# An attention and two feed-forward layers on one core: kept columns for the softmax sums, a third PSUM tile for first products, and second matmuls three chunks behind

## The chip, the cores and the metric

The kernel runs on one core of a Trainium2 chip. The metric is the device time of one execution in microseconds (us), and lower is better. The profile's engines are PE (TensorE matmuls), PEld (its weight loads), DVE (VectorE), ACT (ScalarE), POOL (GpSimd) and SP (SyncE, which issues nearly all DMAs).

## The reference

Three steps follow each other. Attention over 4 batches, 8 heads, 576 tokens and 64 dimensions is the sum of two parts: an attention among averages of 4 tokens, repeated 4 times, and a local one in which a token sees those less than 4 away. Its output, 2304 tokens by 512, goes through two feed-forward layers with 2048 hidden values.

```python
q_d = q.reshape(B, H, Sd, factor, D).mean(axis=3)        # the same for k and v; factor = 4
out_up = np.repeat(sm_attn(q_d, k_d, v_d), factor, axis=2)
mask = np.abs(pos[:, None] - pos[None, :]) < factor
scores = np.where(mask, scale * np.matmul(q, k.transpose(0, 1, 3, 2)), -1000000000.0)
out_local = np.matmul(softmax(scores), v)                # sums get + 1e-09 before the division
x = (out_up + out_local)                                 # as [2304, 512]
h = x @ w_in;  g = np.where(h > 0.0, h, np.exp(np.minimum(h, 0.0)) - 1.0);  x = g @ w_out
h = x @ w_in2; g = s * np.maximum(h, 0.0) ** 2 + b;                         out = g @ w_out2
```

## The kernel before

**Feed-forward.** Both layers are cut into 9 blocks of 256 tokens (j) and 16 chunks of 128 hidden values (f). `ffn_h` computes a chunk's first product, 12 matmuls into a PSUM tile `h` (line 875). ACT, DVE, ACT and POOL then make the nonlinear value as a high part `gh` and a low part `gl`: in layer 1 a Relu and an Exp on ACT (L895, L897), a combination on DVE that reads `h` again (L899), the rounding `gh` on ACT and the rest `gl` on POOL or DVE (L300 is the helper line of every tensor_tensor that may run on either). `ffn_x` multiplies `gh` and `gl` with the second weight, 12 matmuls of 256 columns in layer 1 (L931), 6 of 512 in layer 2 (L934), into two PSUM tiles `acc` that gather over the 16 chunks of a block. `LAG = 2` sets how many chunks the second product comes behind the first. Each weight chunk is loaded as 1 MB in a 64-bit form and converted on DVE, ACT and POOL (L346, L351, L353, L292, L300).

**PSUM.** Of eight tiles, two are `at` (attention), two are `h`, four are `acc`. An `h` tile is free again when DVE's L899 has read it.

**Attention.** A unit is a batch and a pair of heads. Units of batch 0 run before the feed-forward starts, their second half and batch 1 beside the first blocks, batches 2 and 3 (whose local part is done row by row on POOL and DVE, L300, L790 to L819) beside the middle blocks. A unit takes transposes on PE (L512), scores (L550, L639), exponentials on ACT that also give the sums (L571, L667), the reciprocal of the sum on DVE (L577 and L578; L685 and L686; L808 and L809), a multiplication on POOL or DVE, transposes (L595, L698) and the products with v (L612, L713). The averages of v are added on PE in batch 0 (`vsum_pe`, L527) and on POOL or DVE elsewhere (`vsum`, L536 and L537).

**The order of the work.** [...] Where the planner sees PE without work for more than a fraction of a microsecond, it writes filler matmuls into an unused PSUM tile (`keep_warm`, L1135). The constants T0 to VP, GROUP, SWITCH, HOLD and WAIT set due times and choices. For layer 1, blocks 0 and 1 run interleaved at the pace at which weights arrive, blocks 2 to 6 one after the other, blocks 7 and 8 interleaved.

```python
copy(self.vd, ps, 4 * D, r=[ps], w=[self.vd], u=self.tdv, due=due)    # end of vsum_pe
op("dve", 0.29, d2, r=[sm], w=[s4, rs], due=due)                      # sum + 1e-9, times 4; reciprocal
drain(LAG + (ph == 0 and j < 2))
```

Of the kernel before, what the change touches and what calls it, by code (L numbers as in the profile page):

```python
# [16 lines left out]
QB = 96  # L17
# [7 lines left out]
NLP = 3  # L25
# [29 lines left out]
class Plan:  # L55
# [6 lines left out]
    GROUP = 9.0  # L62
    SWITCH = 0.024
    HOLD = 0.089
    WAIT = 1.512
# [162 lines left out]
def attn_moe_moe2(ctx, tc, q, k, v, w_in, w_out, w2_in, w2_out, s2, b2, mask, mask_d, out):  # L228
# [33 lines left out]
    ring = [p1.tile([QB, NQB, 2, D], F32, name=f"p{i}") for i in range(NLP)]  # L262
    nbufs["ring"] = NLP
# [110 lines left out]
    class Unit:  # L374
# [147 lines left out]
        def vsum_pe(self, due):  # L522
            ps = self.ps([G, 4, D], "acc")

            def pe():
                for r in range(4):
                    nc.tensor.matmul(ps(), lhsT=ident[:G, :G], rhs=self.vg()[:, :, r * D:(r + 1) * D],  # L527
                                     start=(r == 0), stop=(r == 3))

            op("pe", 1.9, pe, r=[self.vg], w=[ps], u=self.both, due=due)  # L530
            copy(self.vd, ps, 4 * D, r=[ps], w=[self.vd], u=self.tdv, due=due)

        def vsum(self, due):
            def f(e):
                vg = self.vg()
                e.tensor_tensor(out=vg[:, :, 0:2 * D], in0=vg[:, :, 0:2 * D], in1=vg[:, :, 2 * D:4 * D], op=ALU.add)  # L536
                e.tensor_tensor(out=self.vd(), in0=vg[:, :, 0:D], in1=vg[:, :, D:2 * D], op=ALU.add)  # L537

            op(("pool", "dve"), (2.1, 1.3), (lambda: f(nc.gpsimd), lambda: f(nc.vector)),
               r=[self.vg], w=[self.vg, self.vd], due=due, lock=True)  # L540

        def gs(self, heads, halves, due):
# [11 lines left out]
            nm, sm, s4, rs = (Buf(p2, t, [G, N2, 1]) for t in ("gnm", "gsm", "gs4", "grs"))  # L554
# [25 lines left out]
            op("dve", 0.29, d2, r=[sm], w=[s4, rs], due=due)  # L580
# [4 lines left out]
        def gpt_(self, heads, halves, due):  # L585
# [14 lines left out]
            copy(pt, ps, 2 * n * m * G, r=[ps], w=[pt], due=due)  # L600
# [46 lines left out]
        def softmax(self, pss, half, due):  # L647
            F = 2 * NQB
            n = F * SW
            sc = Buf("ring", "p", None)  # L650
            sc.ring = ring
            part = lambda a: sc()[:, :, a, :SW]
            every = lambda: sc().rearrange("p m a w -> p (m a) w")[:, :, :SW]
            mx, sm, rs = (Buf(p2, t, [QB, F, 1]) for t in ("lmx", "lsm", "lrs"))

            by_act = self.b == 0 and self.hp % 2 < ACT_EXP
            for a, ps in enumerate(pss):
                h = slice(a, F, 2)
                if by_act:
# [22 lines left out]
            def d2():  # L682
                if not by_act:
                    nc.vector.tensor_reduce(out=sm()[:, :, 0], in_=every(), axis=AX.X, op=ALU.add)
                nc.vector.tensor_scalar(out=rs(), in0=sm(), scalar1=1e-9, scalar2=None, op0=ALU.add)  # L685
                nc.vector.reciprocal(out=rs(), in_=rs())  # L686

            op("dve", 0.29 if by_act else 0.5 + n / 960, d2, r=[sc, sm], w=[sm, rs], due=due)
# [16 lines left out]
        def lpv(self, half, due):  # L705
# [10 lines left out]
            op("pe", 0.75, pe, r=[self.vwp[half], self.lpt[half]], w=[ps], u=self.both, due=due)  # L716
# [26 lines left out]
    def direct(b, t, due):  # L743
# [32 lines left out]
        sc = Buf(p2, "ds", [128, 4, 7])  # L776
# [8 lines left out]
        def scores(j):  # L785
# [5 lines left out]
                out=sc()[:, j:j + 2], in_=x(), axis=AX.X, op=ALU.add), r=[x], w=[sc], due=due)  # L791
# [11 lines left out]
        op("dve", 0.35, d1, r=[sc, c_sb2], w=[sc, mx], due=due)  # L803
        op("act", 0.2, lambda: nc.scalar.activation(out=sc(), in_=sc(), func=ACTF.Exp, scale=SCALE), r=[sc], w=[sc], due=due)

        def d2():
            nc.vector.tensor_reduce(out=sm()[:, :, 0], in_=sc(), axis=AX.X, op=ALU.add)
            nc.vector.tensor_scalar(out=sm(), in0=sm(), scalar1=1e-9, scalar2=None, op0=ALU.add)  # L808
            nc.vector.reciprocal(out=sm(), in_=sm())  # L809
            nc.vector.tensor_tensor(out=sc(), in0=sc(), in1=bc(sm), op=ALU.mult)  # L810

        op("dve", 0.75, d2, r=[sc], w=[sc, sm], due=due)

        def values(j):
# [3 lines left out]
               r=[vo, sc], w=[x], u=[rows_], due=due)  # L818
# [45 lines left out]
    def ffn_h(ph, j, f, n=N):  # L864
        due = vt(ph, j, f)
        ps = Buf(ps_h, "h", [128, n])
# [12 lines left out]
        us = 0.0075 + n / 2311  # L879
# [10 lines left out]
        gh, gl = Buf(p3, "gh", [128, n], F32R), Buf(p3, "gl", [128, n], F32R)  # L890
# [3 lines left out]
        if ph == 0:  # L894
            op("act", ta, lambda: nc.scalar.activation(out=e(), in_=ps(), func=ACTF.Relu, scale=-1.0),  # L895
# [300 lines left out]
```

## Time and profile before

| | before |
|---|---|
| median of 3 runs | 994.69 us (989.42 to 995.15) |
| the profiled execution: time | 995.36 us |
| its span, first to last instruction | 993.6 us |
| PE busy in the span | 965.5 us (97%) |
| DVE, ACT, POOL busy | 634.1, 472.2, 405.1 us |
| mean granted TensorE clock | 0.985 |
| filler matmuls (L1135) | 588 |

The span falls into five stretches: from the start to the first matmul of the feed-forward (0 to 52.3 us), layer 1's blocks 0 and 1 (to 227.1), its blocks 2 to 6 (to 484), its blocks 7 and 8 (to 582.2), and layer 2 with the last store (to 993.6). A busy PE is not a PE that does useful work: filler matmuls count, and so do matmuls at half the clock.

### The profile page before, as it was taken

The page shows a single profiled execution, that of the slowest core. Times are in us where ns is not written, and L with a number is a line of the kernel's source. Part 1 is how long each engine was busy: PE and PEld are TensorE (multiplying, and loading weights), DVE is VectorE, ACT ScalarE, POOL GpSimd, SP SyncE. Part 2 cuts the span into 40 slices and gives each one's busy share as a digit, 9 for nine tenths or more (in the row PEclk, how much of TensorE's full clock was granted, in tenths as well). Part 3 has the DMA queues.
Part 4 walks back from the last instruction along what each step waited for, and adds up shares of the span by engine and source line. Part 5 has one row for each costly group of instructions (what it writes and reads, how often), then busy time and mean ns, then how long its engine had stood idle before and what let it go on. Part 6 is the DMA issues. An engine that isn't in the chain of part 4 may idle for free.

```text
span 993.6 us, 21541 instructions
## 1 busy us (share of the span) xinstructions
PE 965.5 (97%) x8480; PEld 893.2 (90%) x8480; DVE 634.1 (64%) x1112; ACT 472.2 (48%) x1227; POOL 405.1 (41%) x358
## 2 busy tenths in 40 slices
PE   8999899998999999999999999999999999999998
PEld 6798888988989989999999999999999999999997
DVE  3478978888898989999637788433333343434332
ACT  4567566436444455444666675433333333333332
POOL 1245554688677787778465563100000000000000
PEclk8599999999999999999999999999999999999999
DMA  9556566435443353333335354001001010100000
GB/s 209 107 150 165 143 180 176 122 108 157 111 105 92 89 132 95 86 106 108 103 105 171 114 169 143 22 1 43 20 25 35 10 43 1 44 1 22 1 23 21
DMA packets 102469, 88.35 MB, mean 89 GB/s; under 512 B 48864, under 2 KB 91872, under 8 KB 102368
## 3 DMA queue, kind: packets, MB, share of 16 engines
q1 hardware_dynamic: 100576, 86.54, 31.4%
q8 instruction: 66, 1.08, 0.5%
q10 hardware_dynamic: 1792, 0.44, 0.2%
q14 instruction: 35, 0.29, 0.1%
HBM read 73.85 MB, written 13.11 MB: 88 GB/s over the span
## 4 chain that ended last, share of the span: by engine, by line
PE 48%; issue 3%; POOL 3%; DVE 3%; ACT 1%; SPq 0%; DMA 0%; POOLq 0%; DVEq 0%; ACTq 0%
PE h L875 24%; PE acc L934 20%; PE acc L931 4%; POOL gl L300 1%; POOL wu L300 1%; POOL w L300 1%; DVE raw L819 1%; DVE raw L351 1%; DVE r L899 0%; ACT raw L292 0%; DVE raw L353 0%; ACT r L895 0%; ACT w L292 0%; DVE wu L300 0%; ACT r L897 0%
## 5 line engine op out<-in xcount | busy, mean ns | idle before, releaser
L875 PE MATMUL h<-x,w 128*128 128x256 f32 x3264 | 430.6, 281 | 13.1 <-DVE r L899 10.8
L875 PEld LDWEIGHTS h<-x,w 128*128 128x128 f32 x3264 | 408.0, 188 | 30.7 <-DVE r L899 13.7
L931 PE MATMUL acc<-gh,w 128*128 128x256 f32 x1152 | 186.1, 283 | 0.0
L934 PE MATMUL acc<-w,gh 128*128 128x512 f32 x576 | 181.0, 395 | 0.0
L931 PEld LDWEIGHTS acc<-gh,w 128*128 128x128 f32 x1152 | 155.0, 188 | 2.5 <-issue 2.3
L905 DVE SCALAR_TENSOR_TENSOR r<-r,sb,h 128x256 f32<-128x256 f32 x144 | 68.8, 479 | 129.7 <-ACT r L904 128.6
L300 POOL TENSOR_TENSOR x<-xr,x 128x256 fp32r<-128x256 f32 (+2 forms) x43 | 43.1, 1021 | 264.0 <-DVE x L294 256.3
L300 POOL TENSOR_TENSOR gl<-r,gh 128x256 fp32r<-128x256 f32 x118 | 113.5, 967 | 59.3 <-ACT gh L292 52.5
L910 DVE SCALAR_TENSOR_TENSOR gl<-r,sb,gh 128x256 fp32r<-128x256 f32 x144 | 73.9, 513 | 99.2 <-ACT gh L908 99.2
L908 ACT ACTIVATE gh<-r,sb 128x256 fp32r<-128x256 f32 x144 | 73.4, 510 | 98.5 <-PE acc L934 89.4
L904 ACT ACTIVATE r<-h 128x256 f32<-128x256 f32 x144 | 55.1, 383 | 134.9 <-PE h L875 133.9
L931 PE MATMUL acc<-gl,w 128*128 128x256 f32 x576 | 114.4, 280 | 0.3 <-POOL gl L300 0.3
L934 PE MATMUL acc<-w,gl 128*128 128x512 f32 x288 | 114.0, 396 | 0.0
L934 PEld LDWEIGHTS acc<-w,gh 128*128 128x128 f32 x576 | 98.2, 188 | 14.1
L895 ACT ACTIVATE r<-h 128x256 f32<-128x256 f32 x144 | 54.7, 380 | 96.5 <-PE h L875 47.2
L300 POOL TENSOR_TENSOR w<-raw,w 128x512 fp32r<-128x512 f32 x47 | 64.2, 1379 | 78.7 <-ACT w L292 74.1
L899 DVE SCALAR_TENSOR_TENSOR r<-r,h 128x256 f32<-128x256 f32 x144 | 58.0, 412 | 49.4 <-ACT r L897 47.2
L931 PEld LDWEIGHTS acc<-gl,w 128*128 128x128 f32 x576 | 87.8, 188 | 0.9 <-POOL gl L300 0.7
L292 ACT ACTIVATE gh<-r 128x256 fp32r<-128x256 f32 x144 | 58.2, 413 | 52.6 <-DVE r L899 32.7
L934 PEld LDWEIGHTS acc<-w,gl 128*128 128x128 f32 x288 | 54.0, 188 | 13.0
L300 POOL TENSOR_TENSOR wu<-raw 128x896 f32<-128x896 f32 x29 | 61.5, 2135 | 9.3 <-DVE raw L819 9.3
L819 DVE TENSOR_REDUCE raw<-wu 128x128 f32<-128x896 f32 x36 | 63.5, 1783 | 2.1 <-POOL wu L300 2.0
(136 smaller groups left out, 1149.3 us busy)
## 6 DMA issues: line engine op xcount, KB each, us to landing
raw<-in_moe_w_in_dram SPq DMA_DIRECT2D x32, 512.0 KB
raw<-in_moe_w_out_dram SPq DMA_DIRECT2D x32, 512.0 KB
raw<-in_k_dram SPq DMA_DIRECT2D x17, 320.0 KB
raw<-in_v_dram SPq DMA_DIRECT2D x17, 320.0 KB
x2d<-ev SPq DMA_DIRECT2D x18, 256.0 KB
xr<-x2d SPq DMA_DIRECT2D x18, 256.0 KB
out_dram<-ev SPq DMA_DIRECT2D x16, 256.0 KB
vg<-in_v_dram SPq DMA_DIRECT2D x12, 288.0 KB
```

What stands on the lines that cost most here:

```text
L292: a = (0.11 + n / 1200, lambda: nc.scalar.activation(out=out(), in_=src(), func=ACTF.Copy, scale=scale))
L300: f = lambda e: lambda: e.tensor_tensor(out=out(), in0=in0(), in1=in1(), op=alu)
L819: op("dve", 0.07 + 14 * D / 546, lambda: nc.vector.tensor_reduce(out=vo()[:, WD + j * D:WD + (j + 2) * D].rearrange("p (j d) -> p j d", j= ...
L875: nc.tensor.matmul(ps(), lhsT=w()[:, wpart, 0, c * 128:(c + 1) * 128], rhs=x()[:, xpart, c, :], start=first and i == 0, stop=last and i == ...
L895: op("act", ta, lambda: nc.scalar.activation(out=e(), in_=ps(), func=ACTF.Relu, scale=-1.0), r=[ps], w=[r1], u=[e], due=due)
L899: op("dve", td, lambda: nc.vector.scalar_tensor_tensor(out=e(), in0=e(), scalar=-1.0, in1=ps(), op0=ALU.add, op1=ALU.max), r=[r2, ps], w=[ ...
L904: op("act", ta, lambda: nc.scalar.activation(out=e(), in_=ps(), func=ACTF.Relu), r=[ps], w=[r1], u=[e], due=due)
L905: op("dve", td + 0.07, lambda: nc.vector.scalar_tensor_tensor(out=e(), in0=e(), scalar=sb2[:, 0:1], in1=ps(), op0=ALU.mult, op1=ALU.mult), ...
L908: op("act", ta + 0.1, lambda: nc.scalar.activation(out=gh(), in_=e(), func=ACTF.Identity, bias=sb2[:, 1:2]), r=[r2], w=[gh], u=[e], due=due)
L910: op("dve", td + 0.07, lambda: nc.vector.scalar_tensor_tensor(out=gl(), in0=e(), scalar=sb2[:, 1:2], in1=gh().bitcast(F32), op0=ALU.add, o ...
L931: nc.tensor.matmul(acc()[:, c * N:(c + 1) * N], lhsT=wo[:, cc * 128:(cc + 1) * 128], rhs=g(), start=(f == 0 and i == 0 and c == 0), stop=l ...
L934: nc.tensor.matmul(acc(), lhsT=g()[:, a * 128:(a + 1) * 128], rhs=wo, start=(f == 0 and i == 0), stop=last)
```

## The change

Five things change. The rows of PE, DVE and POOL behind the words were read from the instruction lists that both programs build.

- The sums of the softmaxes are written into column 0 of tiles of two columns (`gsm`, `lsm`), or lie beside a column that nothing else writes (`ds`, `p`). The kept column holds 1e-9 from the start. One tensor_reduce over both replaces the tensor_scalar that added 1e-9 (L577, L685, L808 go, L580 and others come). The factor 4 moves into a copy (`scale=0.25`), and the scaling of the negative maximum moves from DVE (L563) to ACT (L569).
- Batch 0's averages of v move from PE (`vsum_pe`, L527) to POOL or DVE (`vsum`).
- In blocks 2 to 6 of layer 1, for f of 3, 6, 9 and 12, the first product goes into an `acc` tile in place of an `h` tile.
- `LAG` is 3 in place of 2, and `gh`, `gl` have four buffers in place of three.
- The planner's constants are others, and tiles `p` of the local softmax are two in place of three.

```diff
-T0, P0, LB, TR, R0, P1, P2 = 39.33, 5.045, 7, 29.37, 2.362, 2.546, 2.787
+T0, P0, LB, TR, R0, P1, P2 = 39.86, 4.909, 5, 35.22, 2.175, 2.551, 2.783
...
-    GROUP = 9.0
-    SWITCH = 0.024
+    GROUP = 18.61
+    SWITCH = 0
...
+    rings = {"p": [p1.tile([QB, NQB, 2, D], F32, name=f"p{i}") for i in range(NLP)],
+             "gsm": [p1.tile([G, 2, 2], F32, name=f"gsm{i}") for i in range(2)],
+             "lsm": [p1.tile([QB, 2 * NQB, 2], F32, name=f"lsm{i}") for i in range(2)],
+             "ds": [p1.tile([128, 4, 8], F32, name=f"ds{i}") for i in range(2)]}
...
             def d2():
-                nc.vector.tensor_scalar(out=s4(), in0=sm(), scalar1=1e-9, scalar2=4.0, op0=ALU.add, op1=ALU.mult)
+                nc.vector.tensor_reduce(out=s4()[:, :, 0], in_=sm()[:, :N2], axis=AX.X, op=ALU.add)
                 nc.vector.reciprocal(out=rs(), in_=s4())
...
+                    if j == 0 and sc != 1.0:
+                        nc.scalar.activation(out=nm(), in_=nm(), func=ACTF.Copy, scale=sc)
...
-        ps = Buf(ps_h, "h", [128, n])
+        third = ph == 0 and 2 <= j < NSUB - LASTP and 3 <= f < FC - 3 and f % 3 == 0
+        ps = Buf(ps_a, "acc", [128, n]) if third else Buf(ps_h, "h", [128, n])
...
-        gh, gl = Buf(p3, "gh", [128, n], F32R), Buf(p3, "gl", [128, n], F32R)
+        gh, gl = Buf(p4, "gh", [128, n], F32R), Buf(p4, "gl", [128, n], F32R)
...
-            u.gs((0, 1), first, d), u.ls(0, d), u.vsum_pe(d + VP)
+            u.gs((0, 1), first, d), u.ls(0, d), u.vsum(d + VP)
...
-    LAG = 2
+    LAG = 3
```

Three places on PE show what the new order does. The first lies in the start, about 14 us into the run: `w_224` and `w_287` hold v of the first and second unit, other `w` tiles hold batch 0's q, k and what is made of them. Before:

```order
L698 MATMUL at<-ident,p_85 128x96 x3
L527 MATMUL acc<-w_224,ident 72x256 x4
L550 MATMUL acc<-w_293 72x144 x2
L512 MATMUL at<-ident,w_150 128x96 x3
...
L512 MATMUL at<-ident,w_150 128x96 x3
L527 MATMUL acc<-w_287,ident 72x256 x4
L595 MATMUL h<-ident,s 72x72 x4
```

The rows L527 are gone, the second unit's scores (L550) have moved ahead of what stood before L527, and a few fillers stand where the list waits for the next unit. The same place, changed:

```order
L523 MATMUL at<-ident,w_163 128x96 x6
L550 MATMUL acc<-w_303 72x144 x2
L598 MATMUL h<-ident,s 72x72 x4
...
L699 MATMUL at<-ident,p_85 128x96 x3
...
L1139 MATMUL h<-wz 128x128
...
L550 MATMUL acc<-w_374 72x144 x2
```

The second place is the passage from blocks 0 and 1 to block 2, whose first matmuls use the weight chunk `w_702` before and `w_840` in the changed list. Before:

```order
L713 MATMUL at<-pt,vw 64x32 x18
L502 MATMUL at<-ident,nat 128x72 x4
L931 MATMUL acc<-gh,w_3150 128x256 x4
L931 MATMUL acc<-gl,w_3150 128x256 x2
L550 MATMUL at<-d 72x144 x4
L875 MATMUL h<-x,w_702 128x256 x12
L875 MATMUL h<-x,w_855 128x256 x12
```

In the changed list the second products of block 1 are all done earlier, and fillers (L1139) stand between the attention's matmuls in their place, 81 ahead of block 2's first matmul and 20 within its first chunk:

```order
L935 MATMUL acc<-gh,w_3055 128x256 x4
L935 MATMUL acc<-gl,w_3055 128x256 x2
...
L1139 MATMUL acc<-wz 128x128
...
L714 MATMUL at<-pt,vw 64x32 x18
L513 MATMUL at<-ident,nat 128x72 x4
...
L550 MATMUL at<-d 72x144 x4
...
L879 MATMUL h<-x,w_840 128x256 x8
```

The third place is in the middle of block 2. In the changed list every third first product goes to `acc`, so that the next product into the same `h` tile comes one chunk later:

```order
L879 MATMUL acc<-x,w_1813 128x256 x12
L550 MATMUL at<-d 72x144 x4
L935 MATMUL acc<-gh,w_904 128x256 x4
...
L879 MATMUL h<-x,w_1955 128x256 x12
...
L879 MATMUL h<-x,w_2090 128x256 x12
...
L879 MATMUL acc<-x,w_2232 128x256 x12
```

The second product comes later too: that of block 2's second chunk (`w_904`) stands behind the first product of the seventh chunk (`w_1813`), and before it (`w_855`) stood behind that of the sixth.

Counts in the two lists, of filler matmuls: ahead of the first feed-forward matmul 153 before and 187 changed; from there to the first second product 61 and 76; from there to block 2's first matmul 315 and 155; behind it 59 and 142. Tensor_tensor rows of the helper line: 309 on POOL and 88 on DVE before, 323 and 74 changed.

## Rows read from the trace of the kernel before

**Rows 1.** The page: span and busy time of each engine.
```profile
span 993.6 us, 21541 instructions
PE 965.5 (97%) x8480; PEld 893.2 (90%) x8480; DVE 634.1 (64%) x1112; ACT 472.2 (48%) x1227; POOL 405.1 (41%) x358
```
**Rows 2.** Busy time by stretch: length, engines, PEclk, DMA share, GB/s.
```profile
0.00:52.30 52.30, 49.35 (x598) 38.55 (x599) 22.13 (x64) 26.34 (x104) 12.20 (x23) 0.71 0.75 165
52.30:227.10 174.80, 165.28 (x2306) 152.77 (x2304) 145.11 (x279) 103.90 (x294) 103.92 (x96) 1.00 0.54 145
227.10:484.00 256.90, 247.91 (x2143) 239.64 (x2142) 232.53 (x362) 126.24 (x370) 194.39 (x157) 1.00 0.42 110
582.20:993.60 411.40, 407.37 (x2624) 367.81 (x2622) 170.95 (x332) 154.12 (x334) 35.29 (x34) 1.00 0.10 34
```
**Rows 3.** PE's timeline in layer 2: start, length, instruction.
```profile
702.41 1.56 PE L875 MATMUL h<-x,w 128*128 128x256 f32 x12
...
705.21 1.56 PE L875 MATMUL h<-x,w 128*128 128x256 f32 x12
```
**Rows 4.** PE's timeline in the start.
```profile
14.92 3.48 PE L527 MATMUL acc<-w,ident 72*72 72x256 f32 x8
...
26.43 2.13 PE L713 MATMUL h<-pt,w 38*64 38x32 f32 x36
...
42.89 3.78 PE L1135 MATMUL at<-wz 128*128 128x128 bf16 x40
...
52.33 0.95 PE L875 MATMUL h<-x,w 128*128 128x256 f32 x6
...
58.75 0.71 PE L931 MATMUL acc<-gh,w 128*128 128x256 f32 x4
```
**Rows 5.** Stretches of one granted clock in the start; columns as in rows 2.
```profile
15.50:45.70 30.20, 30.20 (x295) 21.48 (x294) 12.39 (x38) 15.87 (x68) 7.13 (x10) 0.50 0.70 155
45.70:58.75 13.05, 13.05 (x225) 12.35 (x224) 6.81 (x11) 5.82 (x18) 4.97 (x7) 1.00 0.48 162
```
**Rows 6.** Groups by line: instructions, busy us, mean ns, idle before.
```profile
L527 PE MATMUL acc<-w,ident 72*72 72x256 f32 x32 | 14.4, 631 | 0.0
L536 POOL TENSOR_TENSOR vg<-vg 72x512 f32<-72x512 f32 x10 | 15.6, 1558 | 0.0
L537 POOL TENSOR_TENSOR vd<-vg 72x256 f32<-72x256 f32 x10 | 9.2, 921 | 1.1 <-PE at L612 0.4
```
**Rows 7.** PE's timeline between 90 and 96 us: fillers at the full clock.
```profile
92.40 3.08 PE L1135 MATMUL at<-wz 128*128 128x128 bf16 x52
95.31 0.42 PE L698 MATMUL at<-ident,p 96*128 96x96 f32 x3
```
**Rows 8.** PE's waits from 52 to 582 us: total, times, longest.
```profile
PE h L875 <- DVE r L899: 10.8, 15, 2.3
PE at L698 <- POOL p L300: 3.7, 4, 1.3
```
**Rows 9.** The same waits on DVE between 227 and 484 us alone.
```profile
PE h L875 <- DVE r L899: 7.5, 10, 2.3
```
**Rows 10.** Lines on DVE and one on ACT: ns of one as least, median, most.
```profile
L577 DVE TENSOR_SCALAR gs<-gsm x32: 144/577/1559, 12.1 to 410.2; 72x2 f32<-72x2 f32 x32
L801 DVE TENSOR_TENSOR ds<-ds,dmx x18: 186/188/1128, 193.6 to 465.2; 128x28 f32<-128x28 f32 x18
L807 DVE TENSOR_REDUCE dsm<-ds x18: 167/176/183, 194.3 to 465.9; 128x4 f32<-128x28 f32 x18
```
**Rows 11.** Groups by line: ACT's first step of a chunk, and what it waited for.
```profile
L895 ACT ACTIVATE r<-h 128x256 f32<-128x256 f32 x144 | 54.7, 380 | 96.5 <-PE h L875 47.2 <-POOL gl L300 40.0 <-DVE gl L300 6.5
```
**Rows 12.** The timeline from the last product for block 2's tokens to its first matmul.
```profile
212.26 1.24 PE L713 MATMUL at<-pt,vw 38*64 38x32 f32 x36
...
224.74 0.71 ACT L292 ACTIVATE x<-xr 128x256 fp32r<-128x256 f32 x2
...
227.10 3.30 PE L875 MATMUL h<-x,w 128*128 128x256 f32 x24
```

More of the change, by code (lines that the diff above doesn't have):

```diff
@@ L261, in attn_moe_moe2, with kept @@
     msk = p1.tile([QB, 2, NQB, SW], BF16, name="msk")
-    ring = [p1.tile([QB, NQB, 2, D], F32, name=f"p{i}") for i in range(NLP)]
-    nbufs["ring"] = NLP
+    rings = {"p": [p1.tile([QB, NQB, 2, D], F32, name=f"p{i}") for i in range(NLP)],
+             "gsm": [p1.tile([G, 2, 2], F32, name=f"gsm{i}") for i in range(2)],
+             "lsm": [p1.tile([QB, 2 * NQB, 2], F32, name=f"lsm{i}") for i in range(2)],
+             "ds": [p1.tile([128, 4, 8], F32, name=f"ds{i}") for i in range(2)]}
+    for tag, tiles in rings.items():
+        nbufs[tag] = len(tiles)
+    def kept(tag):
+        b = Buf(tag, tag, None)
+        b.ring = rings[tag]
+        return b
     mskd = p1.tile([128, 2, 28], BF16, name="mskd")
@@ L553, in gs @@
             op("pe", 0.25 * N2 / len(heads) + 0.1, pe, r=[self.d], w=pss, u=self.tdv, due=due)
-            nm, sm, s4, rs = (Buf(p2, t, [G, N2, 1]) for t in ("gnm", "gsm", "gs4", "grs"))
+            nm, s4, rs = (Buf(p2, t, [G, N2, 1]) for t in ("gnm", "gs4", "grs"))
+            sm = kept("gsm")
             e = Buf(p2, "s", [G, N2, 2 * G])
@@ L682, in d2 @@
             def d2():
-                if not by_act:
-                    nc.vector.tensor_reduce(out=sm()[:, :, 0], in_=every(), axis=AX.X, op=ALU.add)
-                nc.vector.tensor_scalar(out=rs(), in0=sm(), scalar1=1e-9, scalar2=None, op0=ALU.add)
+                x = sm() if by_act else sc().rearrange("p m a w -> p (m a) w")[:, :, :SW + 1]
+                nc.vector.tensor_reduce(out=rs()[:, :, 0], in_=x, axis=AX.X, op=ALU.add)
                 nc.vector.reciprocal(out=rs(), in_=rs())
-            op("dve", 0.29 if by_act else 0.5 + n / 960, d2, r=[sc, sm], w=[sm, rs], due=due)
+            op("dve", 0.34 if by_act else 0.34 + n / 960, d2, r=[sc, sm] if by_act else [sc], w=[rs], due=due)
             tt(every, every, lambda: rs().to_broadcast([QB, F, SW]), ALU.mult, n, r=[sc, rs], w=[sc], due=due)
@@ L917, in ffn_x @@
         w = w_b[ph, f]
-        due = vt(ph, j, f) + 2 * (P1 if ph == 0 else P2)
+        due = vt(ph, j, f) + 3 * (P1 if ph == 0 else P2)
         if f == 0:
@@ L1140, in attn_moe_moe2 @@
         nc.vector.memset(wz, 0.0)
-        for t in ring:
+        for t in rings["p"]:
             nc.gpsimd.memset(t, 0.0)
+        for t in rings["gsm"] + rings["lsm"] + rings["ds"]:
+            nc.gpsimd.memset(t, 1e-9)
+        for t in rings["p"]:
+            nc.gpsimd.memset(t[:, :, :, SW:SW + 1], 1e-9)
         make_identity(nc, ident)
```

72 lines of the change are left out of this document (33 added, 39 removed).

## The prediction

> **What bounds the kernel now.** I read the page first, then the busy times by stretch, PE's timeline and last its waits. The page has PE busy 97% of 993.6 us [rows 1], which says little, since fillers count. Layer 2 says more: a chunk starts every 705.21 − 702.41 = 2.80 us [rows 3], its 144 chunks make 403 us, and the stretch from 582.2 us holds nearly nothing else. There PE is the bound and nothing in the change shortens it; the last 4 us are the last store. So whatever comes or goes lies in the first 582 us. Layer 1's 144 chunks cost PE the same 403 us there; the other 179 us are the start (52.3 us), attention matmuls, fillers and waits.
>
> In the start PE is never idle from 15.5 us on, but at half the clock: 30.2 us at a granted 0.50 [rows 5]. Four groups of L527 lie there, 14.4 us together [rows 4, 6]. In blocks 0 and 1 DVE is busy 145.1 and POOL 103.9 of 174.8 us, PE runs many fillers, and the pace is that of the chains through DVE, ACT and POOL [rows 2]. In blocks 2 to 6 PE and DVE are close together, 247.9 and 232.5 of 256.9 us [rows 2]; what PE waits for there is DVE's L899, which frees the `h` tile: 7.5 us in 10 waits [rows 9].
>
> **The change part by part.** Its own base is the profiled execution, 995.36 us (1.76 us around its span); the median of the runs shown is 994.69 us, 0.7 lower. I take the two as one.
>
> *Averages of v off PE.* 14.4 us of matmuls leave the start [rows 6]. They lay on the path: PE had no idle time between 15.5 us and the first second product at 58.75 [rows 4, 5]. Against that the new list has 34 more fillers ahead of the first feed-forward matmul and 15 more from there to the first second product. At half the clock a filler costs 3.78 / 40 = 0.095 us [rows 4], so 49 of them give back 4.6, and 9.8 us is the most that PE alone can win. Those fillers mark places where the list waits for the softmax chain, and a chain through ACT, DVE and POOL is not sped up by a PE that is free earlier; the least is nothing. I take 6 us, nearer to PE's sum, because PE's row has no gap at all there. What replaces L527 is a pair on POOL of 1.56 + 0.92 us [rows 6], four times; POOL is busy 12.2 of the first 52.3 us [rows 2], so it is hidden. Without that cover each pair would cost up to 2.5 us.
>
> *The order in blocks 0 and 1.* From the first second product to block 2 the fillers fall from 315 to 155. At the full clock 52 take from 92.40 to 95.31, 0.056 us each [rows 7]: 160 × 0.056 = 9.0 us less. Behind that they rise from 59 to 142: 83 × 0.056 = 4.6 us more, most of it at the passage to block 2. A filler's time is a wait that the list foresaw; where the wait is still there, it comes back under another name (below). Ends: 0 and 9.0; I take all of it and count new waits apart.
>
> *The passage to block 2.* Before, 227.10 − 212.26 = 14.8 us lie between the last product for block 2's tokens and its first matmul [rows 12], with second products and attention in between. In the new list I count some 12.3 us of PE work and fillers there (L713 at 1.24 us, second products at 0.7 us a half chunk, 81 fillers). If the way through the store, the reload and the split needs all of 14.8, PE waits 2.5 us; if it was slack, nothing. I take 1.2 us more.
>
> *Kept columns.* L577 has a median of 577 ns and a least of 144, a tensor_reduce of like size 176 and never more than 183 [rows 10]. 32 of them save about 32 × (0.57 − 0.18) = 12 us of DVE, and 50 instructions of the same kind go from other softmaxes. DVE ran nearly full beside PE, so this is slack rather than time: no term by itself. The 16 scalings that move to ACT are small, and ACT is busy 472 of 993.6 us [rows 1].
>
> The list also moves 14 tensor_tensors from DVE to POOL, 194.4 of 256.9 us busy in blocks 2 to 6 [rows 2]. Here a row speaks against the change: L801, a tensor_tensor of 28 elements, takes 186 ns or up to 1128 [rows 10], so something holds it too. [...]
>
> *Third tile and LAG.* In blocks 2 to 6 an `h` tile is now needed again after three first products in place of two for most chunks, that is 2.8 us later, and the longest wait on L899 was 2.3 us [rows 9]. Of the 7.5 us I take 5 as gone, since the first and last chunks of a block still have two tiles; ends 0 and 7.5. The waits outside, 10.8 − 7.5 = 3.3 us [rows 8, 9], stay. `LAG = 3` alone is nothing: PE hardly waits for `gl`, and in layer 2 the matmuls stay the same.
>
> *New waits.* An order with other neighbours brings waits of its own; PE's others were 3.7 us on POOL's `p` and a few more [rows 8]. With fewer fillers to stand in front of them I add 2 us, from 0 to 9 (all of the fillers' gain).
>
> Sum: −6 − 9.0 + 4.6 + 1.2 − 5 + 2 = −12.2 us. 995.4 − 12.2 = 983.2, so 983 us.
>
> **The rivals.**
> - *The start stays.* The softmax chain, not PE, sets the first feed-forward matmul. For it: the new fillers stand between attention rows. Against it: no idle time on PE from 15.5 to 58.75 us. 983 + 6 = 989 us.
> - *The third tile does nothing*, the change then not doing what it says: ACT's L895 waited 40.0 us for POOL's `gl`, since `r` has two buffers [rows 11], and that limit stays. Against it: PE's waits are put down to L899, not to L895. 983 + 5 = 988 us.
> - *Fillers become waits.* The pace in blocks 0 and 1 is that of weights and softmaxes, and 9.0 us come back as idle time. DVE's 145 of 174.8 us speak against a full bound. 983 + 9 = 992 us less the 2 already counted, 990.
> - *The clock stays up.* If PE keeps the full clock through the start, the 30.2 us at 0.50 shrink; L713 takes 1.24 in place of 2.13 us [rows 4, 12]. After L527's removal some 16 us of half-clock work are left, half of which is 8 us: 975 us.
> - *The clock stays down: slower.* The granted clock fell at 15.5 us, after a PE with gaps, and came back at 45.7, behind L527 and 40 fillers without a gap [rows 4, 5]. With L527 gone PE has more gaps, and the clock may come back only in block 0, or fall again. Each microsecond at half the clock costs half a microsecond of PE's work; from 24 us more of it the 12 us are eaten, and if it lasted through the first half of blocks 0 and 1 (40 us more) the time is 983 + 20 = 1003 us. Against it: 36 and 37 fillers stand at the first feed-forward matmuls, and from 45.7 us on the clock never fell. [...]
>
> **How the numbers follow.** Forecast 0.45 (977 to 988); the start stays 0.13; the third tile does nothing 0.12; fillers become waits 0.10; the clock stays up 0.10; the clock stays down 0.10. The range 972 to 992 takes in all but the last and the outer parts of the bounds. One per cent, about what a measurement of this kernel can tell from no change, is 984.7 to 1004.6. Faster by more takes seven tenths of the forecast (0.32), the clock that stays up (0.10) and a tenth of the other rivals (0.04): 0.46. Slower by more is the half of the last rival that lasts longest: 0.05. Within it the rest, 0.49.
>
> **What would show it.** First second product near 52 to 53 us in place of 58.75. No PE row of `vsum`, four POOL pairs ahead of 30 us. Fillers in PE's stretch of blocks 0 and 1 halved, and idle time there not up by more than 3 us. The wait on the DVE line of the combination, 7.5 us in blocks 2 to 6, down to 2 or 3. The tensor_reduce on `gsm` at about 0.17 us with no spread. An idle time ahead of block 2's first matmul under 3 us. Wrong it would be made by a clock that comes back after 55 us, or by blocks 2 to 6 that take longer than 257 us.

## The result, and the profile after

The changed kernel takes 977.49 us (median of 4 runs, 976.09 to 980.28), the kernel before beside it 992.06 (4 runs, 985.87 to 995.15): a ratio of 0.9852 with a 95% interval of 0.9804 to 0.9900, 1.5% faster. About half of the gain goes with the clock, as the experiments show. The forecast was 983 us, in a range of 972 to 992. The profiled execution after takes 976.13 us against 995.36 before, 19.2 less.

The page after, span and busy time [rows 1]:

```profile
span 974.0 us, 21374 instructions
PE 955.4 (98%) x8420; PEld 892.2 (92%) x8420; DVE 612.4 (63%) x1058; ACT 473.0 (49%) x1239; POOL 409.2 (42%) x385
```

PE loses 10.1 us of busy time and 9.5 us of idle time, DVE 22 us of busy time. Next, busy time by stretch after, with the columns of [rows 2]: the start, blocks 0 and 1, blocks 2 to 6, and what follows the first second product of layer 2 (its first matmul, where the last row of [rows 2] begins, is at 555.97 us here).

```profile
0.00:35.20 35.20, 31.98 (x601) 28.14 (x602) 20.72 (x59) 24.07 (x105) 17.01 (x36) 1.00 0.99 202
35.20:204.30 169.10, 161.89 (x2232) 150.00 (x2230) 143.11 (x258) 108.86 (x310) 103.83 (x98) 1.00 0.58 162
204.30:453.00 248.70, 247.01 (x2118) 240.75 (x2115) 210.21 (x338) 123.00 (x364) 189.13 (x159) 1.00 0.40 105
566.77:974.00 407.23, 403.17 (x2546) 363.62 (x2544) 164.51 (x319) 147.89 (x318) 32.58 (x36) 1.00 0.10 33
```

The start is 17.1 us shorter and its granted clock 1.00 in place of 0.71; blocks 0 and 1 are 5.7 shorter, blocks 2 to 6 8.2, with PE's idle time there down from 9.0 to 1.7 us; in blocks 0 and 1 it falls from 9.5 to 7.2. PE's timeline after, at the places of [rows 4] and [rows 3], and the clock of the stretches of [rows 5]:

```profile
24.44 1.24 PE L714 MATMUL h<-pt,w 38*64 38x32 f32 x36
...
35.20 0.96 PE L879 MATMUL h<-x,w 128*128 128x256 f32 x6
...
43.40 0.73 PE L935 MATMUL acc<-gh,w 128*128 128x256 f32 x4
...
694.43 1.60 PE L879 MATMUL h<-x,w 128*128 128x256 f32 x12
...
697.27 1.60 PE L879 MATMUL h<-x,w 128*128 128x256 f32 x12
```
```profile
15.50:45.70 30.20, 29.09 (x524) 25.83 (x518) 21.94 (x48) 20.61 (x86) 18.02 (x20) 1.00 0.87 205
45.70:58.75 13.05, 12.15 (x243) 11.08 (x243) 9.61 (x24) 11.09 (x44) 5.43 (x6) 1.00 0.31 106
```

Two things stand here that the prediction's sum did not hold. The granted clock stays at 1.00 up to the last matmul (970 us; 0.56 in the last 2 us of the span, when PE has none): the local products with v take 1.24 us, not 2.13. And a chunk of layer 2 takes 697.27 − 694.43 = 2.84 us, not 2.80.

The first second product of layer 1 and the first of layer 2 cut both executions into three, and the next fence gives the middle part, layer 1, from the kernel before and from the one after (length, then PE busy):

```profile
58.75:590.06 531.31, 510.19 (x5245) 488.34 (x5242) 444.37 (x720) 295.60 (x797) 360.67 (x303) 1.00 0.46 126
```
```profile
43.40:566.77 523.37, 512.52 (x5179) 493.19 (x5177) 420.59 (x674) 298.19 (x811) 353.16 (x310) 1.00 0.45 127
```

The start gives 58.75 − 43.40 = 15.35 us and layer 1 7.94. What follows takes 4.06 back (995.36 − 590.06 = 405.30 before, 976.13 − 566.77 = 409.36 after): together 19.2. In layer 1 PE's idle time falls by 10.3 us (21.1 to 10.9) and its fillers from 374 to 297, which is 4.3 us at 0.056; yet its busy time rises by 2.3, so 6.6 us of work came from elsewhere. Over 144 chunks that is 0.046 us each, about as much as a chunk of layer 2 loses: the matmuls of layer 1 seem slower too, which e6 bears out below.

PE's waits in layer 1 after, as in [rows 8], and the lines that took the place of [rows 6] and [rows 10]: averages of v on POOL, the sum over kept columns, and the two on `ds` (ns as least, median, most):

```profile
PE h L879 <- DVE r L903: 3.7, 7, 0.8
PE at L699 <- POOL p L311: 2.4, 5, 0.8
```
```profile
L536 POOL TENSOR_TENSOR w<-w x4: 1261/1263/1266, 9.1 to 22.5; 72x512 f32<-72x512 f32 x4
L537 POOL TENSOR_TENSOR w<-w x4: 722/725/788, 10.4 to 23.9; 72x256 f32<-72x256 f32 x4
L580 DVE TENSOR_REDUCE gs<-gsm x32: 131/144/155, 12.8 to 378.7; 72x2 f32<-72x4 f32 x32
L804 DVE TENSOR_TENSOR ds<-ds,dmx x18: 186/197/1173, 174.4 to 444.9; 128x28 f32<-128x28 f32 x18
L810 DVE TENSOR_REDUCE dsm<-ds x18: 159/185/186, 176.2 to 445.4; 128x4 f32<-128x32 f32 x18
```

The wait for DVE falls from 10.8 to 3.7 us and that for `p` from 3.7 to 2.4. POOL's pairs are done by 24.6 us. The sum has lost its spread; L804, the tensor_tensor, has kept its own.

### The profile page after: what moved, and what is told of

It is laid out like the page before. It is cut to its first block, busy times and chain, and to the rows that moved or that the text cites. A ratio compares the mean times of both kernels' runs of the same rounds, so it can differ in the third digit from the quotient of the medians.

```text
span 974.0 us, 21374 instructions
## 1 busy us (share of the span) xinstructions
PE 955.4 (98%) x8420; PEld 892.2 (92%) x8420; DVE 612.4 (63%) x1058; ACT 473.0 (49%) x1239; POOL 409.2 (42%) x385
## 4 chain that ended last, share of the span: by engine, by line
PE 69%; DVE 11%; POOL 6%; issue 6%; DMA 4%; ACT 3%; SPq 1%; POOLq 0%; DVEq 0%; ACTq 0%
PE h L879 31%; PE acc L938 21%; PE acc L935 12%; POOL gl L311 2%; PE acc L879 2%; DVE raw L362 2%; DMA raw<-in_moe_w_out_dram 2%; DVE raw L364 2%; POOL w L311 1%; POOL wu L311 1%; DVE raw L357 1%; DVE w L311 1%; DVE raw L822 1%; DVE r L903 1%; DMA w<-in_k_dram 1%
## 5 line engine op out<-in xcount | busy, mean ns | idle before, releaser
L879 PE MATMUL h<-x,w 128*128 128x256 f32 x3024 | 407.0, 284 | 4.0 <-DVE r L903 2.9
L879 PEld LDWEIGHTS h<-x,w 128*128 128x128 f32 x3024 | 387.0, 188 | 19.1 <-DVE r L903 5.0
L935 PE MATMUL acc<-gh,w 128*128 128x256 f32 x1152 | 188.8, 285 | 0.0
L935 PEld LDWEIGHTS acc<-gh,w 128*128 128x128 f32 x1152 | 157.3, 189 | 2.6 <-issue 1.9
L311 POOL TENSOR_TENSOR x<-xr,x 128x256 fp32r<-128x256 f32 (+2 forms) x47 | 40.9, 892 | 262.5 <-DVE x L305 254.6
L914 DVE SCALAR_TENSOR_TENSOR gl<-r,sb,gh 128x256 fp32r<-128x256 f32 x144 | 77.8, 541 | 101.8 <-ACT gh L912 101.8
L908 ACT ACTIVATE r<-h 128x256 f32<-128x256 f32 x144 | 55.0, 382 | 130.2 <-PE h L879 129.8
L311 POOL TENSOR_TENSOR w<-raw,w 128x512 fp32r<-128x512 f32 x48 | 66.5, 1397 | 60.3 <-ACT w L303 55.8
L903 DVE SCALAR_TENSOR_TENSOR r<-r,h 128x256 f32<-128x256 f32 x124 | 50.7, 414 | 54.3 <-ACT r L901 49.3
L899 ACT ACTIVATE r<-h 128x256 f32<-128x256 f32 x124 | 46.8, 378 | 66.3 <-PE h L879 39.0
L901 ACT ACTIVATE r<-r 128x256 f32<-128x256 f32 x144 | 60.0, 417 | 3.9
```

The source lines that it names most:

```text
L311: f = lambda e: lambda: e.tensor_tensor(out=out(), in0=in0(), in1=in1(), op=alu)
L879: nc.tensor.matmul(ps(), lhsT=w()[:, wpart, 0, c * 128:(c + 1) * 128], rhs=x()[:, xpart, c, :], start=first and i == 0, stop=last and i == ...
L901: op("act", ta, lambda: nc.scalar.activation(out=e(), in_=e(), func=ACTF.Exp, scale=-1.0), r=[r1], w=[r2], u=[e], due=due)
L903: op("dve", td, lambda: nc.vector.scalar_tensor_tensor(out=e(), in0=e(), scalar=-1.0, in1=ps(), op0=ALU.add, op1=ALU.max), r=[r2, ps], w=[ ...
L914: op("dve", td + 0.07, lambda: nc.vector.scalar_tensor_tensor(out=gl(), in0=e(), scalar=sb2[:, 1:2], in1=gh().bitcast(F32), op0=ALU.add, o ...
L935: nc.tensor.matmul(acc()[:, c * N:(c + 1) * N], lhsT=wo[:, cc * 128:(cc + 1) * 128], rhs=g(), start=(f == 0 and i == 0 and c == 0), stop=l ...
```

## The experiments

**How times are compared.** The time of every version moves with the mean granted clock of its run. In 57 runs of the kernel before beside the experiments, ten with a mean clock of 0.996 or more have a median of 984.67 us, 31 between 0.980 and 0.990 one of 995.06, and seven below that one of 999.01: 7.6 us for each hundredth. So the table gives the median of all runs, the ratio to those runs of the kernel before that stood beside them (4, 17 or 23 runs), and beside it the median of the runs with 0.996 or more ("clock up").

| kernel | median, us (runs) | ratio, 95% interval | clock up, us (runs) | layer 2, us per chunk |
|---|---|---|---|---|
| before | 994.80 (57) | | 984.67 (10) | 2.80 |
| after | 977.49 (4) | 0.9852 [0.9804, 0.9900] | 976.11 (2) | 2.84 |
| e1 two behind in layer 2 | 979.91 (6) | 0.9878 [0.9823, 0.9933] | 977.00 (3) | 2.84 |
| e2 no third tile | 978.32 (6) | 0.9876 [0.9816, 0.9935] | 977.54 (3) | 2.84 |
| e3 one sum as before | 978.41 (6) | 0.9865 [0.9813, 0.9917] | 977.22 (4) | 2.84 |
| e4 averages on PE | 989.97 (12) | 0.9973 [0.9935, 1.0011] | 987.00 (5) | 2.84 |
| e5 tiles moved by 32 bytes | 973.70 (6) | 0.9849 [0.9803, 0.9895] | 973.70 (6) | 2.82 |
| e6 tiles moved by 192 bytes | 972.76 (6) | 0.9824 [0.9771, 0.9876] | 967.09 (2) | 2.80 |
| e7 before, averages on POOL | 989.03 (12) | 0.9977 [0.9939, 1.0016] | 985.49 (5) | 2.80 |
| e8 before, more fillers | 988.80 (12) | 0.9989 [0.9956, 1.0021] | 987.76 (5) | 2.80 |
| e9 before, tiles moved | 1000.55 (12) | 1.0050 [1.0015, 1.0086] | 991.87 (1) | 2.84 |
| e10 r alone moved by 192 | 975.99 (6) | 0.9829 [0.9785, 0.9873] | 972.88 (3) | 2.83 |
| e11 e6 with old numbers | 979.37 (6) | 0.9835 [0.9797, 0.9873] | 973.57 (1) | 2.80 |
| e12 e6, two behind in both | 973.07 (6) | 0.9795 [0.9759, 0.9831] | 972.34 (2) | 2.80 |

### Why layer 2 is slower: e1, e5, e6, e9, e10

The first suspect was `LAG`. e1 takes it back in layer 2 alone (and the due times of its second products with it):

```diff
-        drain(LAG + (ph == 0 and j < 2))
+        drain((LAG if ph == 0 else 2) + (ph == 0 and j < 2))
```

> The changed kernel with its second products in layer 2 two chunks behind again (layer 1 keeps three; PE's order is the same up to the end of layer 1). In layer 2 the changed kernel takes 2.84 us per chunk against 2.80 before. Theory A (three behind is what slows the first products there): 2.80 us per chunk again, 144 x 0.04 = 5.8 us less, about 972 us. Rival B (the slower pace comes from where the tiles lie in SBUF, which stays): 2.84 us, about 977 us, no change. Rival C (three behind hides gl): new waits on gl in layer 2, slower than 979 us.

The pace stays. In e1's timeline the row between the first two shown holds two chunks (24 matmuls), so from the first to the second are three chunks:

```profile
696.72 1.60 PE L879 MATMUL h<-x,w 128*128 128x256 f32 x12
...
705.24 1.60 PE L879 MATMUL h<-x,w 128*128 128x256 f32 x12
...
708.08 1.12 PE L879 MATMUL h<-x,w 128*128 128x256 f32 x8
```

From 696.72 to 705.24 are 8.52 us, 2.84 for each chunk. Theory A falls. What else differs there is where the tiles lie: the change takes one `p` ring and two small tags out of the pools ahead of them and adds three rings, so that `x` starts at byte 183520 of a partition, before at 184736; that is 224 and 416 bytes behind a multiple of 1024, and `r` lies likewise. e5 and e6 put unused bytes ahead of them, and change nothing else:

```diff
+    pad = p1.tile([128, 8], F32, name="pad")     # e5; e6: [128, 48]
     mskd = p1.tile([128, 2, 28], BF16, name="mskd")
```

> The changed kernel with 32 unused bytes per partition ahead of the tiles of the later pools, so that the tokens' tile x starts at 183552 in place of 183520 (a multiple of 256) and r, gh and gl move with it; every engine's order is the same. Layer 2's slower pace stayed with second products two behind, so LAG isn't its cause. Theory A (where these tiles lie in SBUF sets the pace of the first products): 2.80 us per chunk or less in layer 2 in place of 2.84, about 970 us where the clock holds. Rival B (the place by 32 bytes doesn't matter): 2.84 us and 976 to 978 us.

> As the run before with 192 bytes: x and r come to lie as before the change, 416 bytes behind a multiple of 1024 (x at 183712, before at 184736); gh and gl don't (928 against 160). Theory A1 (the place of x or r): 2.80 us per chunk in layer 2, about 970 us. Theory A2 (the place of gh and gl): 2.84 us, 976 to 978 us, while the shift by 32 may do either. Rival B (not the place, but the four gh and gl): both shifts stay at 2.84 us.

With 192 bytes the chunk is back at 2.80 us, and the profiled execution takes 966.82 us, 9.3 less than after, at nearly the same clock (1.000 and 0.999). e6's timeline and, below it, its layer 1 between the same two marks:

```profile
700.04 1.56 PE L880 MATMUL h<-x,w 128*128 128x256 f32 x12
...
702.84 1.56 PE L880 MATMUL h<-x,w 128*128 128x256 f32 x12
```
```profile
43.38:562.21 518.83, 504.06 (x5179) 484.11 (x5177) 420.32 (x674) 297.75 (x811) 353.34 (x310) 1.00 0.46 129
```

Layer 1 takes 4.5 us less and what follows 4.8 less (966.82 − 562.21 = 404.61 against 409.36). PE's busy time in layer 1 falls by 8.5, but it then waits 3.9 more: part of the slower matmuls had lain over waits. `gh` and `gl` lie 928 bytes behind a multiple of 1024 here and 160 before, so theory A2 falls as far as it says that they alone set the pace. 32 bytes give less than the half, 2.82; from the first to the second of these rows of e5's are five chunks:

```profile
695.86 1.60 PE L880 MATMUL h<-x,w 128*128 128x256 f32 x12
...
709.98 1.60 PE L880 MATMUL h<-x,w 128*128 128x256 f32 x12
```

Two more runs ask whether the place alone does it, and which tile's. e9 moves the tiles of the kernel before to the bad place, e10 moves `r`, `gh` and `gl` of the changed kernel and leaves `x`:

```diff
+    pad = p1.tile([128, 208], F32, name="pad")   # e9, in the kernel before
     mskd = p1.tile([128, 2, 28], BF16, name="mskd")
```
```diff
+                    p2.tile([128, 24], F32, tag="pad", name="pad")   # e10, ahead of the first r
```

> The kernel before, in the same order, with 832 unused bytes per partition ahead of the later pools, so that x and r lie 224 bytes behind a multiple of 1024, as in the changed kernel, in place of 416. Theory A (the change moved x or r to a worse place, and that cost it some 9 us): 2.84 us per chunk in layer 2 in place of 2.80, 990 to 993 us where the clock holds (before: 982.3 at full clock) and 1002 to 1005 at the usual mean clock. Rival B (the place matters only beside what else the change did): 2.80 us, the times of before.

> The changed kernel with 192 unused bytes between x and r: r, gh and gl lie as in the run with all of them moved by 192, x stays at 224 behind a multiple of 1024; same order. Theory A (it is x, which the first products stream): 2.84 us per chunk, 975 to 977 us at full clock. Rival B (it is r): 2.80 us, 966 to 967 us at full clock.

e9's chunks in its timeline, then two of its windows, the last part of the start and layer 1:

```profile
691.89 1.60 PE L876 MATMUL h<-x,w 128*128 128x256 f32 x12
...
694.73 1.60 PE L876 MATMUL h<-x,w 128*128 128x256 f32 x12
```
```profile
30.00:45.70 15.70, 15.02 (x205) 13.91 (x204) 11.05 (x15) 7.62 (x26) 7.84 (x9) 0.78 0.77 182
...
48.77:581.44 532.67, 518.22 (x5245) 497.90 (x5242) 442.12 (x720) 296.26 (x797) 360.62 (x303) 1.00 0.46 125
```

The kernel before gets the slow pace from 832 unused bytes: rival B falls. It costs 4.9 us in what follows layer 1 (991.68 − 581.44 = 410.24 against 405.30). In layer 1 8.0 us more of busy time cover 6.7 of waits; the 1.4 that are left may be clock, since 3.4 us of layer 1 ran at a granted 0.50 there (from 89.0 us).

e10's chunks come next. Below them stand groups of matmuls in layer 1 (100 to 560 us; the second number is the mean ns of one), each time after, e10 and e6: first products, whose operand of 128x256 is `x`, and second products, whose one is `gl`. The weight, 128x128, is loaded by PEld in both (LDWEIGHTS, 188 ns each after).

```profile
693.98 1.60 PE L879 MATMUL h<-x,w 128*128 128x256 f32 x12
...
705.30 1.59 PE L879 MATMUL h<-x,w 128*128 128x256 f32 x12
```
```profile
L879 PE MATMUL acc<-x,w 128*128 128x256 f32 x240 | 32.7, 285 | 0.0
L879 PE MATMUL acc<-x,w 128*128 128x256 f32 x240 | 32.6, 284 | 0.0
L880 PE MATMUL acc<-x,w 128*128 128x256 f32 x240 | 32.0, 282 | 0.0
L935 PE MATMUL acc<-gl,w 128*128 128x256 f32 x534 | 107.2, 282 | 0.0
L941 PE MATMUL acc<-gl,w 128*128 128x256 f32 x534 | 106.0, 279 | 0.0
L936 PE MATMUL acc<-gl,w 128*128 128x256 f32 x544 | 107.8, 279 | 0.0
```

From 693.98 to 705.30 us are four chunks, 2.83 us each, nearer theory A: with `x` unmoved the first products of layer 2 take 1.59 to 1.60 us, as after, and about three quarters of the loss stay. In layer 1 its second products are as fast as e6's (279 ns), while its first ones are nearly as slow as after's (284 and 285). So in these groups each product's pace goes with the place of its operand of 128x256: `x` for the first, `gl` for the second. `x` was not moved alone, and `r`, `gh` and `gl` only together. That the place sets the pace is shown; by what mechanism is not.

### The start, the averages and the clock: e4, e7, e8

e4 puts the averages back on PE in the changed kernel, e7 takes them off PE in the kernel before, and e8 holds them there with fillers ahead:

```diff
-            u.gs((0, 1), first, d), u.ls(0, d), u.vsum(d + VP)
+            u.gs((0, 1), first, d), u.ls(0, d), u.vsum_pe(d + VP)      # e4; e7 the other way round
...
             def pe():
+                for r in range(16):                                     # e8
+                    nc.tensor.matmul(ps().rearrange("p r d -> p (r d)")[:, 0:128], lhsT=wz[:, :G], rhs=wz, start=True, stop=True)
```

> The changed kernel with the averages of v in the first block on PE again (the 32 matmuls and the 4 evictions of before, in an order that the planner makes for it: 106 fillers ahead of the first feed-forward matmul in place of 187). [...] Rival B (the softmax chain sets the start): first feed-forward matmul within 3 us of 35.2, clock at full speed, 977 to 981 us. Rival C (PE's work alone, 7 us at full clock, and no fall of the clock): about 984 us.

> The kernel before with the averages of v in the first block on POOL and nothing else of the change (the planner makes its own list: 201 fillers ahead of the first feed-forward matmul, 578 up to the second sixteen chunks, 708 in all). Theory A (the averages are the change's gain, 8.5 us at full clock by the run that put them back): 973 to 977 us where the clock holds. Rival B (the gain needs the new list of tasks too, since this one has 120 fillers more and they stand for waits): 980 to 985 us where it holds. In both, falls of the clock add up to 10 us; the median is 3 to 6 us above.

> The kernel before with 16 further fillers (bf16, 128 columns, some 0.9 us) ahead of each of the four groups of averages on PE, else in the same order: 3.6 us more work for PE in the start at full clock. Theory A (the clock falls there since PE has gaps and small matmuls, and fillers hold it): mean granted clock 0.995 or more in most runs, in place of 0.985, and 984 to 988 us in place of 995. Rival B (fillers there don't hold the clock): mean clock 0.985 or less, 997 to 1002 us.

e4 is slower by 11 us where the clock is up, nearest rival C, but not by the averages alone. Its first second product is at 47.90 us, 4.5 later than after, of which up to 3.4 are clock (6.8 us at a granted 0.50, from 36.8 us). Its layer 1 takes 582.29 − 47.90 = 534.39 us, 11.0 more than after, with 463 fillers in place of 297 (9.3 us) and 3.4 us at 0.50: the planner (`Plan.emit`, which writes every engine's list ahead, from costs and due times) made another list.

e7 is the other side. Where the clock is up it comes out at 985.49, as before, near its rival B. Its first second product is at 47.06 us. e9, the order of before with as long a stretch at 0.50 in its start (6.8 us), has it at 48.77, so the averages alone give 1.7 us there. e7's list has 49 fillers more in layer 1 (423 for 374), 2.7 us, which is enough to take that back. The window of its layer 1 is 9.1 us longer than before, but most of this may be clock, since 17 us of it ran at 0.50 (its mean clock is 0.98):

```profile
47.06:587.51 540.45, 520.78 (x5293) 497.85 (x5291) 447.25 (x715) 297.59 (x801) 362.29 (x306) 0.98 0.45 126
```

The averages shorten the start; whether layer 1 keeps that is decided by the list.

In most runs of the kernel before the clock falls for long: 38 of 57 have a mean of 0.986 or less. The profiled execution, with 0.985, has its fall in the start [rows 5]; where the others have theirs isn't recorded. e9, with the same order, has such a mean in 8 of 12 runs, and the changed order in 2 of 46 (after, e1, e2, e3, e5, e6, e10 and e12, which on PE are the same up to block 2): so the new order lets the clock fall less often. With e8's fillers none of 12 has it (0.989 to 0.998), and though they add 3 us where the clock is up, the median is 6 us lower: theory A, with the mean clock a little under what it asked for (six of the twelve at 0.995 or more). What stood ahead of a fall can be seen in e7 and e4, in stretches of their windows (length, then PE busy; the clock behind the five engines):

```profile
15.50:20.00 4.50, 3.89 (x101) 3.08 (x99) 3.65 (x15) 4.50 (x29) 3.14 (x4) 1.00 1.05 197
20.00:25.00 5.00, 3.44 (x76) 2.77 (x77) 4.15 (x12) 2.28 (x14) 4.61 (x6) 0.98 1.11 283
25.00:30.00 5.00, 5.00 (x90) 4.85 (x76) 2.63 (x7) 3.75 (x21) 2.66 (x4) 0.50 1.09 273
```
```profile
32.00:34.00 2.00, 0.77 (x14) 0.59 (x11) 1.67 (x5) 1.86 (x2) 0.74 (x2) 1.00 0.58 132
34.00:36.00 2.00, 1.52 (x39) 1.41 (x39) 1.86 (x3) 0.71 (x3) 1.61 (x1) 1.00 0.57 119
36.00:38.00 2.00, 2.00 (x28) 1.66 (x28) 2.00 (x3) 1.41 (x4) 0.52 (x1) 0.70 0.68 153
38.00:40.00 2.00, 2.00 (x31) 1.94 (x30) 0.95 (x3) 1.51 (x4) 1.13 (x1) 0.50 0.07 5
```

In both PE was idle for 1.6 to 1.7 us within the 5 us before its granted clock went from 1.00 to 0.50. e4 runs the same 32 matmuls between 10.7 and 28.5 us at a granted clock of 1.00, so they don't bring the fall by themselves. Nor does every such gap: in the kernel before PE waits 2.3 us in one piece in blocks 2 to 6 [rows 9] and keeps 1.00 [rows 2]. And not all falls lie in the start: e5's profile has 6.8 us at 0.50 from 71.5 us on, e7's 10.2 us from 352.5. What decides from run to run wasn't found.

### The other parts: e2, e3, e11, e12

```diff
-        third = ph == 0 and 2 <= j < NSUB - LASTP and 3 <= f < FC - 3 and f % 3 == 0
+        third = False                                                   # e2
...
-                nc.vector.tensor_reduce(out=s4()[:, :, 0], in_=sm()[:, :N2], axis=AX.X, op=ALU.add)
+                nc.vector.tensor_scalar(out=s4(), in0=sm()[:, :N2, 0:1], scalar1=1e-9, scalar2=None, op0=ALU.add)   # e3
```

> The changed kernel without the third tile for first products; PE's order is the same up to block 2. Theory A (the prediction's, -5 us with ends 0 and -7.5): PE's wait for the DVE combination line, 3.7 us in all, comes back to 8 to 11 us, the time is 980 to 984 us. Rival B (the third tile does nothing, since r has two buffers): 977 to 978.5 us, the wait still under 5 us.

> The changed kernel with the sums of the softmax over group tokens taken by a tensor_scalar again, in the same order on every engine; the kept columns stay for the other two. Theory A (the 12 us of DVE are slack): within 1.5 us of 977.5, while the line's mean goes from about 0.17 us to 0.5 or more. Rival B (DVE's chain paces blocks 0 and 1): 32 x 0.4 = 13 us of DVE come back, at least 4 of them on the path, 981.5 us or more.

Without the third tile PE waits just as long for the DVE line, in fewer and longer waits, and the time is about 1 us up, within what these runs resolve. The planner's list has 16 more fillers in layer 1 (0.9 us), where it foresaw waits. That is rival B, but not its reason: that `r` has two buffers was not tested.

```profile
PE h L879 <- DVE r L903: 3.7, 4, 1.7
```

e3's line takes 505 ns in the median and up to 1966, beside 144 and 155 after, and the time moves by 1 us: theory A, this gain of DVE's is slack (the other two kept columns stay in e3). Its row, and the longest of its sums beside POOL:

```profile
L580 DVE TENSOR_SCALAR gs<-gsm x32: 144/505/1966, 12.8 to 381.7; 72x2 f32<-72x2 f32 x32
...
257.95 2.11 POOL L311 TENSOR_TENSOR wu<-raw 128x896 f32<-128x896 f32 x1
258.12 1.97 DVE L580 TENSOR_SCALAR gs<-gsm 72x2 f32<-72x2 f32 x1
```

It ends at 260.09 us, just behind POOL's instruction (260.06). In e3's trace 19 of the 32 sums take more than 0.2 us, and each of them ends 21 to 26 ns after an instruction of POOL has ended; after, 21 of the 32 tensor_reduces run beside an instruction of POOL, and none takes more than 155 ns.

So at the same place in the same order the tensor_scalar was held and the tensor_reduce was not. In the kernel before it is as in e3: 19 of L577's 32 take more than 0.2 us, and each ends 22 to 29 ns after an instruction of POOL. The tensor_tensor L804 is held after, too: 8 of its 18 take 378 to 1173 ns and end 43 to 50 ns after one. What holds the one form beside POOL and not the other is not shown.

e11 and e12 start from e6. e11 has the planner's constants of before (all of T0 to VP, GROUP, SWITCH, HOLD, WAIT), e12 `LAG = 2` and due times two chunks behind:

```diff
-T0, P0, LB, TR, R0, P1, P2 = 39.86, 4.909, 5, 35.22, 2.175, 2.551, 2.783
+T0, P0, LB, TR, R0, P1, P2 = 39.33, 5.045, 7, 29.37, 2.362, 2.546, 2.787   # e11
...
-    LAG = 3
+    LAG = 2                                                                # e12
```

> The changed kernel with x moved by 192 bytes, and with the planner's numbers of before (the two rows of times and the four costs): averages on POOL, kept columns, third tile and three chunks behind are in. 646 fillers in place of 560. Theory A (the numbers, which set the order, hold much of the gain: the averages alone gave nothing in the old order): 974 to 982 us at full clock in place of 966.6. Rival B (the gain is that of the other parts, which only together do it): 966 to 970 us.

> The changed kernel with x moved by 192 bytes and second products two chunks behind in both layers; third tile and numbers stay, 635 fillers in place of 560. Theory A (three behind alone is worth nothing, as predicted): 966 to 968.5 us at full clock. Rival B (it makes room for the third tile, and both only work together): waits on gl in layer 1, 970 us or more at full clock.

e11 has a median 6.6 us above e6's, of which its lower mean clock (0.9917 against 0.9940) explains some 2 at 7.6 us a hundredth. Its layer 1 takes 575.18 − 48.94 = 526.24 us, 7.4 more than e6's, of which up to 3.4 are clock (6.8 us at a granted 0.50, from 118.7 us). So the numbers are worth some 4 to 5 us, between theory A (974 in place of 966.6, 7 us or more) and rival B (3 or less). e12's layer 1 takes 567.17 − 43.75 = 523.42 us, 4.6 more than e6's, with 372 fillers in place of 297 (4.2 us) and 3.4 us at 0.50 (from 523.9 us, up to 1.7 us of work). Its times don't settle it: the medians are alike (973.07 and 972.76, at like mean clocks), while its fastest run is 971.25 and e6's 966.82. What three behind may give is room for the list in place of fillers, not rival B's waits on `gl`, of which neither profile has any.

## Why the prediction was right, and where it wasn't

The range held and the sign was right, but that 983 came near 977 is in part luck: two omissions, the clock (10 us or more to the good) and the place of the tiles (9.3 us to the bad), nearly cancel.

**Start, −6.** Measured −15.35 by the first second product. e9, the order of before in a run whose clock fell later and more briefly, has it at 48.77: so about 10 us at least are clock. Of the other 5.4 some part is e9's own fall (15.70 × 0.22 = 3.5 us of clock are missing there), so work and order gave 2 to 5.4, less than the term said, 1.7 of it by the averages alone (e7). Whether the list keeps it is another matter.

**The clock.** It was a rival at 0.10 (975 us) when it is the usual case: in all four runs after, the mean is 0.992 or more. The step that failed is the sum itself, made against one execution at 0.985 as if its clock were part of the kernel. The runs shown before, 989.42 and 994.69 to 995.15 us, had the spread that it left unasked. Where the clock is up in both, the change gives 984.67 − 976.11 = 8.6 us, half of the medians' difference (994.80 − 977.49 = 17.3 with all 57 runs); the other half goes with the clock. The opposed rival, a clock that stays down (1003), had the wrong sign. It had a PE with more gaps lose its clock: e4 and e7 agree in that the clock fell behind 1.6 to 1.7 us of idle time; but with the 32 matmuls of L527 out of the start it fell less often (2 of 46 runs, before 38 of 57). Nor did a microsecond at a granted 0.50 cost the half that it counted: a filler took 0.095 us there and 0.056 at 1.00 [rows 4, 7], L713 2.13 and 1.24 [rows 4, 12], which is 0.41 to 0.42.

**"In layer 2 the matmuls stay the same."** The same instructions run 0.04 us per chunk slower. No term held that kept columns and four `gh` and `gl` move every later tile. It took 9.3 us (e6), 4.5 in layer 1 and 4.8 behind it, the largest single loss.

**Fewer fillers, −9.0 and +4.6.** Counted from the first second product, 374 become 297, 4.3 us: the sum −4.4 holds. Its two parts don't. The lists' counts put the fillers right ahead of block 2's first matmul, 81 in the changed list and 8 before, behind it: in the traces 323 become 236 up to that matmul (4.9 us) and 51 become 61 behind it. So the fillers of blocks 0 and 1 were not halved. They did not come back as waits either, as a rival had it: PE's idle time there fell by 2.3 us. **Passage, +1.2:** from the local product with v at 191.55 us, which matches the one at 212.26 in [rows 12], to block 2's first matmul at 204.39 are 12.8 us, before 14.8, and PE has no wait in them; the term is 0.

**Third tile, −5; new waits, +2.** The waits did fall, from 21.1 to 10.9 us of idle time in layer 1, but not by the third tile: e2 waits as long without it, so the rival that it does nothing had the waits right and the time (988) wrong. Some 4 of the 10 us are waits that the slower matmuls cover (14.8 in e6); the other 6 come with the list. The two terms and the passage gave −1.8 for it, some 4 too little. The planner's numbers had no term of their own, and e11 puts some 4 to 5 us on them: the step was mis-sized there. `LAG`, "alone nothing", is 4.6 us of layer 1 in e12's profile, up to 1.7 of it clock, and nothing in its median, which stays open.

**Kept columns, no term.** Right for the one of three that e3 takes back, with the line at 144 ns in place of 577 and no spread; and POOL's pairs of 1.26 + 0.73 us are hidden in the start.

In sum, of the 19.2 us: 15.4 start, mostly clock; 12.5 layer 1 and 0.7 behind it, as e6 has them; less 9.3 for the place.

## What to carry to other kernels

A tuned kernel's edit that adds or drops a small tile moves all that lies behind it, as here `x` from byte 184736 to 183520: compare the pace of the unchanged inner loop before and after, and if it differs, put the tiles back with unused bytes before judging the edit. e6 does so: 967.09 us with the clock up and 972.76 in the median, faster than both. Ask of a profile whether its clock is the kernel's or the run's: half of the medians' difference here goes with a clock that falls less often in the new order. And before a stretch of one profile is compared with the same stretch of another, see that both ran it at the same granted clock.

## What was unexpected of the hardware

The same matmuls, in the same order with the same neighbours, take from 2.80 to 2.84 us per chunk by where the tiles lie in a partition, in steps down to 32 bytes (2.82, e5), in either kernel (e6 2.80, e9 2.84); by e10 each group of layer 1 follows its own operand of 128x256 (279 and 284 ns). A tensor_scalar of 144 ns took up to 1966 beside POOL, and ended 21 to 26 ns behind POOL's instruction each time that it was long (19 of 32 in e3), while the tensor_reduce in its place never took more than 155. And the granted clock is a matter of chance as well as of the program: 57 runs of one program have means from 0.977 to 0.998 and times from 982.36 to 1000.04 us.
